# FNet mixing and product-key experts on Trainium2: the terms of token 512 and of column d = 256 as biases, column sums and GpSimd folds

## The chip, the cores and the metric

The kernel runs on one core of one Trainium2 chip. The metric is device time in microseconds (us) of one execution. Five engines work side by side, each in the order of its own instructions: PE (TensorE, the matrix products), ACT (ScalarE), DVE (VectorE), POOL (GpSimd) and SP (SyncE, which here issues most of the transfers). They wait for each other through semaphores.

## The reference

x is [2048 tokens, 512 channels]. Each token is normalised over its channels (xn); the result is the sum of three parts:

```python
a = einsum("bsd,ed->bse", xn, dft_hid_re);  b = einsum("bsd,ed->bse", xn, dft_hid_im)
y = einsum("ts,bse->bte", dft_seq_re, a) - einsum("ts,bse->bte", dft_seq_im, b)   # real part of a 2-D DFT
q = einsum("nd,dhc->nhc", xn, w_q)            # 32 heads, two halves of 128
s1, s2 = q[..., :128] @ k1.T, q[..., 128:] @ k2.T      # 64 scores each; the 2 best of each
# the 2 best of the 4 sums name two rows of u and v; gate by softmax, gelu(xn . u), times v
return x + y + out
```

## The kernel before, in words

**The DFT part** uses the symmetries of the DFT matrices. Tokens are put in an order in which token n, its mirror images and its partners at a distance of 1024 lie in the same lanes, 16 tiles of 128 tokens, four tiles to a group g; the groups are taken in the order G = (1, 0, 2, 3). Sums and differences of partners (`fold`, L356 to L369) leave for each group a quarter of the rows and half of the columns: `Q[0][g]` (even part, 257 columns) and `Q[1][g]` (odd part). `main` (L380 to L391) multiplies them with a quarter of the sequence matrix (`A`), eight fp32 products of 128x512 per call, four PSUM banks `PP[k]`. `evict` copies the banks to SBUF through `turn` (reordering columns), and `hid` (L458 to L474) later multiplies them with the hidden matrix, one tile of 128 output tokens at a time, while the router runs.

**What does not fit the symmetry.** Token 512 is its own mirror image, so it has no place in the 4 x 128 rows: its two partner rows come as `x5` (one partition, two rows of 512). `fold_row` (L371 to L375) folds them on DVE into `s5` (even) and into row 0 of `Q[1][0]` (odd). In `main`, L391 adds token 512's share to the banks of k = 0, h = 0 as two products with one row (a stationary of 1x128 against the one row `c5r` of the sequence matrix). Column d = 256 does not fit the 256 folded columns: `sides` (L400 to L418) sums its products with the matrix on DVE into `a256` (128 x 2 x 512), `sums` (L532 to L545) sums that over the partitions by a product with a column of ones (`one`), two products of 1x512, and turns the result into the row `p256`. In `hid`, L461 adds the column as a product with one row: `pn` (1x128 of p256) against `wrs` (row 256 of the hidden matrix, 1x129). `hid` then copies the bank to SBUF in five ACT pieces (L465 to L469).

**The router** (`scores`, L735 on) multiplies xn, transposed by `xpose` and split into two fp16 parts, with `M[j]` (w_q times the keys, made by `m_mul`, `m_scale` and `m_parts`), 12 fp16 products of 128x512 per tile and head group (L743), 16 tiles times 8 groups j. ACT evicts a bank (L748), DVE finds the best eight per head (L751) and their places (L755). Into this run the nine `hid` calls are placed by hand (`HID`, one per tile from tile 11 of j = 0). **The expert part** (L872 z, L910 g, L955 v) follows. Beside it, `compare`, `compare_w` and `fit` verify that the matrices given have the symmetries used and that the numbers fit in fp16; their flag decides whether a slower general branch, not run here, follows.

**What sets the order.** The code is written for a tile framework whose scheduler orders each engine's instructions by its own estimate of when they become ready; so each engine's order can differ from the text, and once built it is fixed. In the head the layer norm of a group (`ln`) takes four steps on ACT and DVE: means and variances, `Sqrt` on ACT (L315), the reciprocal and its refinement on DVE (L316 to L320), and the normalising of four tiles, mostly on ACT (L332). The groups follow each other closely, so ACT's Sqrt for one group stands between the normalising of the group before and its own. `m_scale` (L196 to L212) needs the largest magnitudes of the four banks `m0` to `m3`, then a reduction over the partitions on GpSimd (L118), before `m_parts` (L219, L220) can write the fp16 parts that the first scores need.

Of the kernel before, what the change touches and what calls it, by code (L numbers as in the profile page):

```python
# [8 lines left out]
F32 = mybir.dt.float32  # L9
# [6 lines left out]
AF = mybir.ActivationFunctionType  # L16
# [3 lines left out]
P = 128  # L20
# [15 lines left out]
def tile_fnet_peer(ctx, tc, x, ca, cb, c5, wt, wf, wr, wq, kt, ut, vn, out):  # L36
# [56 lines left out]
    sums_sb = cst.tile([P, 138 + NF + 3], F32, name="sums")  # L93
    chk, asum = sums_sb[:, 0:70], sums_sb[:, 70:138]
# [5 lines left out]
    fits = sums_sb[:, 138:]  # L100
# [155 lines left out]
    s5 = da.tile([1, 257], F32, name="s5")  # L256
    for t in Q[1]:
        nc.gpsimd.memset(t[:, :, 0:1], 0.0)
# [79 lines left out]
    def fold_d(k, t, f, o):  # L338
# [8 lines left out]
        nc.vector.tensor_tensor(halves(f)[..., 1:P], halves(t[:, :, 0:256])[..., 0:P - 1],  # L347
                          halves(t[:, :, 256:512])[..., 1:P], op=op)
        c = 256 - P * k
        nc.vector.tensor_tensor(o[:, :, c:c + 1], t[:, :, 127:128], t[:, :, 384:385], op=op)  # L350
        if k == 0:
            nc.scalar.activation(f[:, :, 0:P + 1:P], t[:, :, 255:257], AF.Copy)
        nc.vector.tensor_tensor(o[:, :, k:P], f[:, :, k:P], f[:, :, P + k:], op=op)
        nc.vector.tensor_tensor(o[:, :, P + k:2 * P], f[:, :, k:P], f[:, :, P + k:], op=po)
# [16 lines left out]
    def fold_row(k):  # L371

        r = da.tile([P, 2, 512], F32, tag="ft", name=f"r5_{k}", bufs=1).rearrange("p a c -> p (a c)")[0:1].unsqueeze(1)
        nc.vector.tensor_tensor(r[:, 0, 0:512], x5[:, 0], x5[:, 1], op=ALU.subtract if k else ALU.add)
        fold_d(k, r[:, :, 0:512], r[:, :, 512:768], Q[1][0][0:1, 0:1] if k else s5.unsqueeze(1))  # L375
# [3 lines left out]
    def main(k, g):  # L379

        first, last = g == G[0], g == G[-1]
        if first:
            PP[k] = [[pa(f"p{k}_{dt}{h}") for h in range(2)] for dt in range(2)]
        for h in range(2):
            r = A[k, g][:, h * 512:(h + 1) * 512]
            l = Q[k][g][:, h ^ k]
            for dt in range(2):
                nc.tensor.matmul(PP[k][dt][h], l[:, dt * P:(dt + 1) * P], r, start=first, stop=last and h + k > 0)  # L388
                if last and h > k:

                    nc.tensor.matmul(PP[0][dt][0], s5[:, dt * P:(dt + 1) * P], c5r, start=False, stop=True)  # L391

    def add(dst, a, v, first=False):

        if first:
            nc.vector.tensor_scalar(dst, v, a, None, op0=ALU.mult)
        else:
            nc.vector.scalar_tensor_tensor(dst, v, a, dst, op0=ALU.mult, op1=ALU.add)

    def sides():  # L400


        f = FF["t"][:, 0, 0:4]
        nc.vector.tensor_copy(f[:, 0:2], Q[0][G[0]][:, :, 256])
        nc.vector.tensor_copy(f[:, 2:4], c5s[:, :, G[0]])
        for n, g in enumerate(G):
            for h in range(2):
                add(a256[:, h], Q[0][g][:, h, 256:257] if n else f[:, h:h + 1],
                    A[0, g][:, h * 512:(h + 1) * 512], n == 0)
# [5 lines left out]
        nc.scalar.activation(r[:, 0], c5r, AF.Copy, scale=s5[:, 256:257])  # L415
        nc.scalar.activation(r[:, 1, 0:257], s5, AF.Copy, scale=c55)
        nc.gpsimd.tensor_tensor(a256[0:1, 0], a256[0:1, 0], r[:, 0], op=ALU.add)
        nc.gpsimd.tensor_tensor(a5[0:1, 0], a5[0:1, 0], r[:, 1, 0:257], op=ALU.add)  # L418

    PT = {}  # L420
    p256 = uf[12][0:1].rearrange("p (h t) -> p h t", h=2)
    p5 = uf[13][:, 257:263]
    a256 = uf[0].rearrange("p (h t) -> p h t", h=2)
    a5 = uf[1][:, 0:514].rearrange("p (k d) -> p k d", k=2)

    def turn(dst, src):

        d = dst.rearrange("p (q k c) -> p k q c", q=2, k=4)
        v = src.rearrange("p (k q c) -> p k q c", q=2, k=4)
        nc.scalar.activation(d, v, AF.Copy)  # L430

    def evict(k):
        PT[k] = [[uf[8 + 2 * k + dt][:, h * 512:(h + 1) * 512] for h in range(2)] for dt in range(2)]
        for dt in range(2):
            for h in range(2):
                turn(PT[k][dt][h], PP[k][dt][h])
# [21 lines left out]
    def hid(t, n, pre, pn, pim, bank):  # L458

        nc.tensor.matmul(bank[:n, 0:129], pre[0], wfs[:, 0:129], start=True, stop=False)  # L460
        nc.tensor.matmul(bank[:n, 0:129], pn, wrs, start=False, stop=True)  # L461
# [3 lines left out]
        nc.scalar.activation(t[:, 2:256:2], bank[:n, 0:127], AF.Copy)  # L465
        nc.scalar.activation(t[:, 1:256:2], bank[:n, 129:257], AF.Copy)
        nc.scalar.activation(t[:, 256:258], bank[:n, 127:129], AF.Copy)
        nc.scalar.activation(t[:, 513:514], bank[:n, 127:128], AF.Copy)
        nc.scalar.activation(t[:, 0:1], bank[:n, 128:129], AF.Copy)  # L469
# [14 lines left out]
    nc.scalar.dma_start(c5s, c5)  # L484
    c5r = da.tile([1, 512], F32, name="c5r")
# [7 lines left out]
    wrs = uf[13][0:1, 0:129]  # L493
    nc.sync.dma_start(wrs, wr)
# [4 lines left out]
    for n, g in enumerate(G):  # L499
# [5 lines left out]
        if n == 3:  # L505
            fold_row(0)
        main(0, g)
# [10 lines left out]
    for n, g in enumerate(G):  # L518
        fold(1, g)
        if g == 0:  # L520
            fold_row(1)
            nc.scalar.activation(xp[1][0:1], x5, AF.Copy)
# [9 lines left out]
    def sums():  # L532
        for h in range(2):
            p = pc(f"p256_{h}")[0:1]
            nc.tensor.matmul(p, one, a256[:, h], start=True, stop=True)
            turn(p256[:, h], p)
        b5 = pc("b5")
        for k in range(2):
            for dt in range(3 - k):
                c = slice(dt * P, min((dt + 1) * P, 257))  # L540
                n = P if dt < 2 else 1
                nc.tensor.matmul(b5[:n, 3 * k + dt:3 * k + dt + 1], a5[:, k, c], one, start=True, stop=True)
        nc.scalar.activation(p5.rearrange("p (k d) -> p k d", k=2)[:, :, 0:2],
                             b5[:, 0:6].rearrange("p (k d) -> p k d", k=2)[:, :, 0:2], AF.Copy)
        nc.scalar.activation(p5[0:1, 2:3], b5[0:1, 2:3], AF.Copy)  # L545

    def y_rows(n):

        if n == 8:
            hid(uf[13][0:1, 264:778], 1, [p5[:, dt:dt + 1] for dt in range(2)], p5[0:1, 2:3],  # L550
# [4 lines left out]
        hid(uf[n][:, 0:514], P, [PT[0][dt][h][:, c] for dt in range(2)], p256[:, h, c],  # L555
# [19 lines left out]
    def part_b(safe, stS, stP, stE, xt, u_sb, cmp_p):  # L575
# [401 lines left out]
        def compare(n):  # L977
# [37 lines left out]
            if g == 0:  # L1015
# [4 lines left out]
                elif odd == ri:  # L1020
                    nc.vector.memset(t[0:1, 2, 0:2], 0.0)
# [7 lines left out]
        def compare_w(n):  # L1029


            ri, half = divmod(n - 64, 2)
            t = bp.tile([P, 4, 256], F32, tag="w", name=f"cx{n}", bufs=WB)
# [51 lines left out]
        def verdict():  # L1085
# [4 lines left out]
            fm = sums_sb[:, 138 + NF:]  # L1090
# [3 lines left out]
            cols = ((slice(0, 64), 50), (slice(64, 70), 47))  # L1094
# [7 lines left out]
            nc.gpsimd.partition_all_reduce(fr[:, 2:], sums_sb[:, 138:], P, bass_isa.ReduceOp.absmax)  # L1102
# [32 lines left out]
        if not safe:  # L1135
            nc.vector.memset(chk[:, 68:70], 0.0)
# [249 lines left out]
```

## Time and profile before

| | |
|---|---|
| median of 3 runs | 1166.12 us (1165.64 to 1166.95) |
| the profiled execution | 1165.58 us, of which the span from its first to its last instruction is 1163.7 us |
| busy, share of the span | PE 98%, DVE 80%, ACT 52%, POOL 20% |
| granted TensorE clock, mean | 0.997 |
| head: first instruction to the first score product (L743) | 64.0 us |
| scores (L743): busy PE | 297.3 us in 1344 products |
| z (L872) and v (L955): busy PE | 343.0 us and 338.6 us |

The chain of work that ended last is by 72% PE, 16% DVE and 5% POOL. In the rows of the timeline, a row gives start, duration, engine, line, operation, output <- input with shapes, how many were merged, and in square brackets how long the engine had been idle and what ended that. An fp32 product is recorded as two passes, so "x8" of L388 is four products of 128x512.

### The profile page before, as it was taken

To read this page: it belongs to the slowest core of one execution; us is meant where nothing else is said; L and a number is where in the kernel's file an instruction comes from. 1 tells how busy PE (TensorE), PEld (TensorE's weight loads), DVE (VectorE), ACT (ScalarE), POOL (GpSimd) and SP (SyncE) were. 2 spreads that over 40 slices of the span, in tenths; PEclk is the share of its full clock that TensorE was granted. 3 is DMA by queue.
4 is the path that set the end of the run, shared out by engine and by line. 5 is a ranking of instruction groups with operands and counts; after the bars stand their busy time and mean duration, and the time that the engine had idled before them with its cause. 6 is when DMAs were issued, how large, how long until landed. Compare 5 with 4: busy or idle time off the path is not lost.

```text
span 1163.7 us, 25367 instructions
## 1 busy us (share of the span) xinstructions
PE 1142.7 (98%) x9940; PEld 726.3 (62%) x9940; DVE 933.3 (80%) x2845; ACT 608.4 (52%) x1047; POOL 232.3 (20%) x214
## 2 busy tenths in 40 slices
PE   6999999999999999999999999999999999999997
PEld 4455555445445449878479569569569559658763
DVE  7987889798998998983995896797886887788670
ACT  5674576777876745354435435535526436334440
POOL 2032454765756420000010010010010000000000
PEclk9999999999999999999999999999999999999999
DMA  9171334243341204260653653644545555452423
GB/s 366 62 284 55 117 128 172 82 146 117 102 146 44 86 25 129 69 221 20 218 177 111 210 170 135 196 158 162 185 158 173 167 172 168 155 163 60 143 74 103
DMA packets 81296, 163.64 MB, mean 141 GB/s; under 512 B 15876, under 2 KB 31115, under 8 KB 81166
## 3 DMA queue, kind: packets, MB, share of 16 engines
q1 hardware_dynamic: 80864, 161.84, 42.0%
q8 instruction: 80, 1.31, 0.5%
q14 instruction: 50, 0.41, 0.1%
q10 hardware_dynamic: 302, 0.08, 0.0%
HBM read 142.68 MB, written 17.63 MB: 138 GB/s over the span
## 4 chain that ended last, share of the span: by engine, by line
PE 72%; DVE 16%; POOL 5%; ACT 3%; issue 2%; DMA 1%; SPq 0%; POOLq 0%; ACTq 0%; DVEq 0%
PE v L955 28%; PE z L872 27%; PE s L743 8%; DVE vals L751 5%; DVE idx L755 4%; PE g L910 4%; POOL wq L165 1%; PE p L388 1%; DVE m L220 1%; DVE z L694 1%; DVE z L693 1%; POOL wq L166 1%; POOL u L634 1%; PE m L144 1%; ACT wh L158 0%
## 5 line engine op out<-in xcount | busy, mean ns | idle before, releaser
L872 PE MATMUL z<-xb,u 128*128 128x256 f16 (+1 forms) x3840 | 343.0, 251 | 1.3 <-ACT act L879 1.2
L955 PE MATMUL v<-v,act 128*128 128x512 f16 x1536 | 338.6, 379 | 0.0
L872 PEld LDWEIGHTS <-u 128*128 128x128 f16 x3840 | 309.8, 98 | 28.0 <-issue 1.7
L743 PE MATMUL s<-m,xq 128*128 128x512 f16 x1344 | 297.3, 379 | 0.0
L955 PEld LDWEIGHTS <-act 128*128 128x128 f16 x1536 | 147.3, 98 | 171.0
L743 PEld LDWEIGHTS <-xq 128*128 128x128 f16 x1344 | 129.6, 98 | 150.4 <-issue 0.2
L900 DVE TENSOR_TENSOR L<-io_lam,cmp 128x2048 f16<-128x2048 f16 x128 | 155.7, 1217 | 61.8 <-PE g L910 61.8
L879 ACT ACTIVATE act<-z,scl 128x256 f32<-128x256 f32 (+1 forms) x224 | 100.8, 498 | 172.3 <-PE z L872 172.2
L751 DVE MAX8 vals<-ss 128x8 f32<-128x64 f32 x1024 | 152.7, 216 | 20.1 <-ACT ss L748 19.9
L968 POOL TENSOR_TENSOR y<-y,xr 128x512 f32<-128x512 f32 x15 | 27.5, 1836 | 610.9 <-DMA y<-y_d 459.3
L925 ACT ACTIVATE act<-w 128x1024 f16<-128x1024 f32 x52 | 69.6, 1354 | 93.0 <-DVE w L918 92.4
L755 DVE FIND_INDEX8 idx<-vals,ss 128x8 uint16<-128x256 f32 x256 | 107.2, 419 | 0.0
L918 DVE SCALAR_TENSOR_TENSOR w<-act,scl,g 128x1024 f32<-128x1024 f32 x64 | 81.0, 1274 | 29.7 <-ACT act L879 29.7
L748 ACT ACTIVATE ss<-s,wsc 128x512 f32<-128x512 f32 x112 | 74.5, 679 | 49.1 <-PE s L743 39.7
L1027 ACT ACTIVATE cx<-cx 128x896 f32<-128x896 f32 x64 | 60.5, 946 | 74.0 <-DVE cx L1011 54.0
L926 DVE TENSOR_TENSOR act<-w,act 128x1024 f16<-128x1024 f32 x64 | 86.0, 1346 | 4.1 <-ACT act L925 4.1
L1005 DVE TENSOR_TENSOR cx<-cx 128x512 f32<-128x512 f32 (+2 forms) x84 | 48.4, 610 | 24.0 <-DMA cx<-in_cb_dram 23.1
L910 PEld LDWEIGHTS <-L 128*128 128x128 f16 x2048 | 60.6, 96 | 11.2 <-DVE R L908 1.3
L910 PE MATMUL g<-R,L 128*128 128x32 f16 x2048 | 61.7, 176 | 0.3 <-DVE R L908 0.2
L908 DVE TENSOR_TENSOR R<-R,cmp 128x512 f16<-128x512 f16 x128 | 59.6, 465 | 1.5
L166 POOL TENSOR_TENSOR wq<-wq,wh 128x1024 f16<-128x1024 f32 x26 | 55.4, 2132 | 11.1 <-DVE xq L456 7.2
L905 DVE TENSOR_TENSOR R<-io_c,cmp 128x512 f16<-128x512 f16 x128 | 53.3, 416 | 0.0
(285 smaller groups left out, 1081.4 us busy)
## 6 DMA issues: line engine op xcount, KB each, us to landing
v<-v_d SPq DMA_DIRECT2D x67, 512.0 KB, 4.1
cx<-in_cb_dram SPq DMA_DIRECT2D x64, 448.0 KB, 4.5
wq<-in_wq_dram SPq DMA_DIRECT2D x32, 512.0 KB, 5.4
fit<-in_wq_dram SPq DMA_DIRECT2D x28, 512.0 KB, 5.1
uv<-in_vn_dram SPq DMA_DIRECT2D x16, 512.0 KB, 3.8
uv<-in_ut_dram SPq DMA_DIRECT2D x16, 512.0 KB, 5.8
c<-in_ca_dram SPq DMA_DIRECT2D x8, 512.0 KB, 11.2
y<-y_d SPq DMA_DIRECT2D x16, 256.0 KB, 2.6
```

Source lines behind the costliest of these rows:

```text
L743: nc.tensor.matmul(ps, xt[i][:, l, kd, :], m[:, r, kd, :], start=(n == 0), stop=(n == 3 * KD - 1))
L748: nc.scalar.activation(s.rearrange("p g e -> p (g e)"), ps, AF.Copy, scale=inv)
L751: nc.vector.max(vals[:, i, w, :, h], s[:, g, :])
L755: nc.vector.max_index(idx[:, i, w].rearrange("p k h -> p (k h)"), vals[:, i, w, 0:2].rearrange("p k h -> p (k h)"), s[:, w * HC:g + 1, :]. ...
L872: nc.tensor.matmul(ps if n == 1 else ps.rearrange("p (b n) -> p b n", b=2), ug[:, l, c % 2, kd, :], xb2[:, k0, r, kd, :] if n == 1 else xb ...
L879: nc.scalar.activation(ACT[bb][:, cg * m:cg * m + m, :], pv[:, i], AF.Gelu_apprx_tanh, scale=zsc)
L900: nc.vector.tensor_tensor(L.rearrange("p t (l two) -> p t l two", two=2), io_lam.rearrange("p (l two) -> p l two", two=2).unsqueeze(1).to_ ...
L910: nc.tensor.matmul(p[:, hf, t * NC:(t + 1) * NC], L[:, t, :], R[:, t, :], start=True, stop=True)
L918: nc.vector.scalar_tensor_tensor(w, act[:, :, ts], fw, p.rearrange("p h (n c) -> p c (h n)", c=NC), op0=ALU.mult, op1=ALU.mult)
L925: nc.scalar.activation(w16[..., 0], w, AF.Copy)
L926: nc.vector.tensor_tensor(w16[..., 1], w, w16[..., 0], op=ALU.subtract)
L955: nc.tensor.matmul(pv, w16[:, c, :, l], v_sb[g][:, r, cc, :], start=(n + cc == 0 and k == 0), stop=(n == 15 and cc == 1 and k == 2))
```

## The change

1. **Token 512 in the evictions.** L391 is gone. The two values of its matrix row that occur (`c52`, a copy of the first two of `c5r`) are multiplied with `s5` on ACT (`spread`, two products of 1x256), written to DRAM (`s5_d`) and read back as columns (`s5c`, 128 x 2 x 2), both by GpSimd's queue. `turn` gets a bias: for the banks of k = 0, h = 0 it runs twice on every other column, as Identity with the bias `s5c`.
2. **Column 256.** `sides` writes the last group's step in the turned order (four steps of 128x256 for two of 128x512) into another tile. `sums` takes eight products with `a256`'s columns as stationary and two columns `w2` (the two values of row 256 of the hidden matrix, loaded to all partitions) as moving operand, into one bank, and evicts it once: `p256` is now a column pair per tile. `hid` loses L461 and adds the pair as bias: six ACT pieces for five, five of them Identity with a bias.
3. **Row folds on GpSimd.** `fold_row` runs on GpSimd, in tiles of its own, for k = 0 and k = 1 one after the other in the text where only k = 0 stood; row 0 of `Q[1][0]` is then copied by DVE from `s5i`.
4. **The verification** covers what is now assumed (that these rows hold two values in turn): four memsets become small additions, and one 1x129 row is loaded and compared, by two DVE steps and one ACT step. One ACT copy (`c52`) now stands first on ACT, with a table load of its own ahead of the one for Sqrt.

```diff
     def fold_row(k):
-        r = da.tile([P, 2, 512], F32, tag="ft", name=f"r5_{k}", bufs=1).rearrange("p a c -> p (a c)")[0:1].unsqueeze(1)
-        nc.vector.tensor_tensor(r[:, 0, 0:512], x5[:, 0], x5[:, 1], op=ALU.subtract if k else ALU.add)
-        fold_d(k, r[:, :, 0:512], r[:, :, 512:768], Q[1][0][0:1, 0:1] if k else s5.unsqueeze(1))
+        r = da.tile([1, 1, 768], F32, tag="r5", name=f"r5_{k}", bufs=1)
+        nc.gpsimd.tensor_tensor(r[:, 0, 0:512], x5[:, 0], x5[:, 1], op=ALU.subtract if k else ALU.add)
+        fold_d(k, r[:, :, 0:512], r[:, :, 512:768], (s5i if k else s5).unsqueeze(1), nc.gpsimd)
+    def spread():
+        for a in range(2):
+            nc.scalar.activation(s5p[:, a].rearrange("o t p -> o (t p)"), s5[:, 0:256], AF.Copy, scale=c52[:, a:a + 1])
+        nc.gpsimd.dma_start(s5_d.rearrange("n p -> (n p)").unsqueeze(0), s5p.rearrange("o a t p -> o (a t p)"))
+        nc.gpsimd.dma_start(s5c.rearrange("p a t -> p (a t)"), s5_d.rearrange("n p -> p n"), allow_slow_non_contiguous=True)
...
-                nc.tensor.matmul(PP[k][dt][h], l[:, dt * P:(dt + 1) * P], r, start=first, stop=last and h + k > 0)
-                if last and h > k:
-                    nc.tensor.matmul(PP[0][dt][0], s5[:, dt * P:(dt + 1) * P], c5r, start=False, stop=True)
+                nc.tensor.matmul(PP[k][dt][h], l[:, dt * P:(dt + 1) * P], r, start=first, stop=last)
...
+        for a in range(2):
+            nc.scalar.activation(d[..., a::2], v[..., a::2], AF.Identity, bias=b[:, a:a + 1])
...
-        nc.tensor.matmul(bank[:n, 0:129], pre[0], wfs[:, 0:129], start=True, stop=False)
-        nc.tensor.matmul(bank[:n, 0:129], pn, wrs, start=False, stop=True)
+        nc.tensor.matmul(bank[:n, 0:129], pre[0], wfs[:, 0:129], start=True, stop=True)
...
-        nc.scalar.activation(t[:, 2:256:2], bank[:n, 0:127], AF.Copy)
+        for d, v, a in ((t[:, 2:256:4], bank[:n, 0:127:2], 0), (t[:, 4:256:4], bank[:n, 1:127:2], 1),
+                        (t[:, 256:258], bank[:n, 127:129], 1), (t[:, 513:514], bank[:n, 127:128], 1),
+                        (t[:, 0:1], bank[:n, 128:129], 1)):
+            nc.scalar.activation(d, v, AF.Identity, bias=pn[:, a:a + 1])
...
+    nc.scalar.activation(c52, c5r[:, 0:2], AF.Copy)
...
-        for h in range(2):
-            p = pc(f"p256_{h}")[0:1]
-            nc.tensor.matmul(p, one, a256[:, h], start=True, stop=True)
-            turn(p256[:, h], p)
+        b8 = pc("b8")
+        for n in range(8):
+            g, q = divmod(n, 2)
+            c = q * 256 + g % 2 * P
+            nc.tensor.matmul(b8[:, 2 * n:2 * n + 2], a256[:, g // 2, c:c + P], w2, start=True, stop=True)
+        nc.scalar.activation(p256, b8[:, 0:16].rearrange("p (n a) -> p n a", n=8), AF.Copy)
```

The scheduler places the new steps as follows. **ACT in the head.** `xb` and `xq_113` are the tiles of group 0 that are being normalised, `ff_0` takes group 2's Sqrt, `nm` a zero for the statistics of group 3. Before:

```order
L332 ACTIVATE xb_109<-xb_109,negm,rstd 128x512
L332 ACTIVATE xq_113<-xq_113,nm_163 128x512
L295 ACTIVATE nm_163<-xq_113 128x1
L315 ACTIVATE ff_0_309<-mvs,eps 128x4
L352 ACTIVATE ff_0_309<-ft_0_328 128x4
L332 ACTIVATE xq_116<-xq_116,negm,rstd 128x512
```

With the change (its own line numbers; L316 is its Sqrt, L385 the two products of `spread`, `r_0` the row fold's tile):

```order
L333 ACTIVATE xb_109<-xb_109,negm,rstd 128x512
L333 ACTIVATE xq_113<-xq_113,nm_164 128x512
L353 ACTIVATE r_0_395<-r_0_395 1x2
L435 ACTIVATE r_628<-c5r,s_156 1x4x2x64
L296 ACTIVATE nm_164<-xq_113 128x1
L385 ACTIVATE s5p<-s_156,c_197 1x256
L385 ACTIVATE s5p<-s_156,c_197 1x256
L436 ACTIVATE r_628<-s_156,c_199 1x257
L316 ACTIVATE ff_0_316<-mvs,eps 128x4
L353 ACTIVATE ff_0_316<-ft_0_335 128x4
L333 ACTIVATE xq_116<-xq_116,negm,rstd 128x512
```

Five ACT steps that read what GpSimd's row fold writes (`r_0`, and `s` for s5) moved ahead of group 2's Sqrt; before, their like stood behind group 3's normalising. **GpSimd** with the change, from the normalising of x5 (before, the reduction of L118 followed it directly):

```order
L336 TENSOR_SCALAR x_162<-x_162,mvs,rstd 1x512
L375 TENSOR_TENSOR r_0_395<-x_162 1x512
L348 TENSOR_TENSOR r_0_395<-r_0_395 1x2x127
L351 TENSOR_TENSOR s_156<-r_0_395 1x1
L354 TENSOR_TENSOR s_156<-r_0_395 1x128
L355 TENSOR_TENSOR s_156<-r_0_395 1x128
L375 TENSOR_TENSOR r_1_406<-x_162 1x512
L355 TENSOR_TENSOR s5i<-r_1_406 1x127
L386 DMA s_d<-s5p 16x1x32
L387 DMA s5c<-s_d 128x4x1
L118 ISA pw_432<-mx_423 128x3
```

(Three rows of the second fold, like those of the first, are left out ahead of its last.) Both folds now stand ahead of the two transfers of s5c. **DVE around group 3's last fold step**, which makes `q_3`, the operand of the last products of k = 0; `ft_1` is the first fold step of k = 1. Before, then with the change:

```order
L354 TENSOR_TENSOR fo_3_379<-ff_3_378 128x2x128
L374 TENSOR_TENSOR r_0_388<-x_161 1x512
L368 TENSOR_TENSOR q_3_151<-fo_3_379 128x257
L369 TENSOR_TENSOR q_3_151<-fo_3_379 128x257
L347 TENSOR_TENSOR r_0_388<-r_0_388 1x2x127
```

```order
L355 TENSOR_TENSOR fo_3_386<-ff_3_385 128x2x128
L366 TENSOR_TENSOR ft_1_454<-xq_114,xq_115 128x1024
L369 TENSOR_TENSOR q_3_151<-fo_3_386 128x257
L370 TENSOR_TENSOR q_3_151<-fo_3_386 128x257
L348 TENSOR_TENSOR ff_1_455<-ft_1_454 128x4x127
```

The step of 128x1024 took the place of the row step of 1x512 ahead of q_3.

More of the change, by code (lines that the diff above doesn't have):

```diff
@@ L92, in tile_fnet_peer @@
     NF = NW + 32 + NCH - 1
-    sums_sb = cst.tile([P, 138 + NF + 3], F32, name="sums")
-    chk, asum = sums_sb[:, 0:70], sums_sb[:, 70:138]
+    sums_sb = cst.tile([P, 139 + NF + 3], F32, name="sums")
+    chk, asum = sums_sb[:, 0:71], sums_sb[:, 71:139]
     wsc = cst.tile([P, 5], F32, name="wsc")
@@ L256, in tile_fnet_peer @@
     s5 = da.tile([1, 257], F32, name="s5")
+    s5i = da.tile([1, 257], F32, name="s5i")
     for t in Q[1]:
@@ L506, in tile_fnet_peer @@
             fold_row(0)
+            spread()
+            fold_row(1)
         main(0, g)
@@ L554, in y_rows @@
         h, c = g // 2, slice(q * 256 + g % 2 * P, q * 256 + g % 2 * P + P)
-        hid(uf[n][:, 0:514], P, [PT[0][dt][h][:, c] for dt in range(2)], p256[:, h, c],
+        hid(uf[n][:, 0:514], P, [PT[0][dt][h][:, c] for dt in range(2)], p256[:, n],
             [PT[1][dt][h][:, c] for dt in range(2)], (pb if q else pc)(f"hy{q}_{g}"))
@@ L1135, in part_b @@
         if not safe:
-            nc.vector.memset(chk[:, 68:70], 0.0)
+            nc.vector.memset(chk[:, 68:71], 0.0)
         for g in range(3):
```

83 lines of the change are left out of this document (55 added, 28 removed).

## The prediction

> **What bounds the kernel now.** I read the page's head first, then the waits, then the head of the program in order of time.
>
> ```profile
> span 1163.7 us, 25367 instructions
> PE 1142.7 (98%) x9940; PEld 726.3 (62%) x9940; DVE 933.3 (80%) x2845; ACT 608.4 (52%) x1047; POOL 232.3 (20%) x214
> PE m L148 <- DMA wq<-in_wq_dram: 8.8, 1, 8.8
> PE p L388 <- DVE q L368: 3.9, 2, 3.3
> DVE vals L751 <- ACT ss L748: 19.9, 20, 3.3
> ```
>
> PE is idle for only 21 us of the span: 8.8 at the start, 3.9 for the folds of the head; most of the rest is the tail after its last product. From the first score at 64 us on it waits for almost nothing. So a PE slot taken out behind 64 us is time won, if DVE follows; DVE waited 19.9 us for the scores' evictions, spread over 20 places, so it has the slack to follow a few us. In the head it is otherwise: PE waits for DVE, and DVE for ACT. So the change has two halves, a gain behind 100 us on PE, and a head whose chain it lengthens.
>
> **The head.** This is the timeline before, rows of POOL, ACT, DVE and PE:
>
> ```profile
> 17.21 4.21 POOL L335 TENSOR_SCALAR x<-x,mvs,rstd 1x512 f32<-1x512 f32 x2 [3.21 <-DVE rstd L319]
> 20.41 0.30 ACT L315 ACTIVATE ff<-mvs,eps 128x4 f32<-128x4 f32 x1
> 21.45 0.17 DVE L316 RECIPROCAL ff<-ff 128x4 f32<-128x4 f32 x1
> 24.39 3.70 PE L388 MATMUL p<-c,q 128*128 128x512 f32 x8 [0.53 <-DVE q L368]
> 31.41 7.91 PE L388 MATMUL p<-c,q 128*128 128x512 f32 x14 [3.32 <-DVE q L368]
> 35.23 0.67 DVE L374 TENSOR_TENSOR r<-x 1x512 f32<-1x512 f32 x1
> 35.83 0.41 DVE L368 TENSOR_TENSOR q<-fo 128x257 f32<-128x257 f32 x1
> 36.29 0.48 PEld L388 LDWEIGHTS p<-c,q 128*128 128x128 f32 x2 [0.38 <-DVE q L368]
> 42.45 7.10 PE L388 MATMUL p<-c,q 128*128 128x512 f32 x16
> 64.03 1.24 PE L743 MATMUL s<-m,xb 128*128 128x512 f16 x5
> ```
>
> GpSimd has x5 normalised at 21.42. ACT takes group 2's Sqrt at 20.41, DVE its reciprocal at 21.45; the products of groups 2 and 3 wait for what follows from it (3.32 and 0.38 us idle). With the change ACT's queue holds five steps ahead of this Sqrt, the last three of which need s5 complete. So the Sqrt cannot come before GpSimd has folded the row. What that takes, by size:
>
> ```profile
> L681 POOL TENSOR_TENSOR c<-vals 128x64 f32<-128x64 f32 x7 | 2.2, 319 | 10.4 <-DVE vals L751 10.4
> L706 POOL TENSOR_TENSOR di<-if 128x128 f32<-128x128 f32 x7 | 3.2, 458 | 0.0
> L418 POOL TENSOR_TENSOR u<-u,r 1x257 f32<-1x257 f32 x1 | 0.7, 718 | 0.0
> L166 POOL TENSOR_TENSOR wq<-wq,wh 128x1024 f16<-128x1024 f32 x26 | 55.4, 2132 | 11.1 <-DVE xq L456 7.2
> L416 ACT ACTIVATE r<-s,c 1x257 f32<-1x257 f32 x1 | 0.5, 493 | 0.0
> ```
>
> From 64 to 128 columns 139 ns are added, 2.2 ns a column, and 128 to 257 agree; so 512, 254, 1, 128 and 128 columns take 1.28, 0.71, 0.18, 0.46 and 0.46 us, 3.1 in all: s5 at 24.5. Then ACT's two products of 1x256 and the one of 1x257 at some 0.4 each from start to start (L416's 0.49 less the overlap of neighbours): Sqrt at 25.8, reciprocal at 26.15, **4.7 us later** than now. Bounds: at L166's 2.1 ns a column without a fixed part the fold takes 2.1 (delay 3.7); at L335's 2.1 us per 512 it takes 4.2 and more (delay 6.2). I take 4.7, the four rows with two operands being nearest. Nothing hides it: DVE's queue stands at this reciprocal, and the normalising of group 2, q_0, q_2 and q_3 are behind.
>
> Group 3's q_3 is another 0.55 later: DVE has the fold of 128x1024 (1.23 a step, some 1.15 from start to start) ahead of it where the row step took 0.60 (35.23 to 35.83). So the last group's products begin at 36.29 + 4.7 + 0.55 = 41.55. From there PE is the bound again, with less to do:
>
> ```profile
> 39.32 1.05 PE p L391 x2
> 40.37 1.06 PE p L388 x2
> 41.43 1.06 PE p L391 x2
> 57.99 0.23 PE xp L452
> 63.31 0.87 PE xp L447 x8
> ```
>
> The chain of waits shows the one-row products at 1.05 and 1.06, both gone. What is left from the last group's first product to the first score: 8 + 32 passes at 0.434 (16 in 6.95, 42.45 to 49.40), 17.4; ten transposed tiles at 0.44 (two of four steps each in the last row's 0.87), 4.4; eight L452 at 0.23, 1.8: 23.6 us. Now it takes 27.74 (36.29 to 64.03) with the 2.1 of L391, so 2.0 are stalls, of which 0.5 lie beside L391. Stepping the new order through ACT and DVE by these rows I find 0.4; between 0.4 and 1.5 I take 1.0. First score at 41.55 + 23.6 + 1.0 = 66.15: **the head loses 2.1 us**; 0.6 less or 0.5 more by the stalls, 1.0 less or 1.5 more by the fold. DVE's own row steps (0.60 for the first of five) are inside this: from 41.55 on PE is the bound, so taking them off DVE wins nothing by itself.
>
> Three new things lie beside it. ACT's first step waits for c5r, then loads a second table; a load is 1.28 us, and the first Sqrt now begins at 7.78:
>
> ```profile
> 7.78 0.30 ACT L315 ACTIVATE sm<-mvs,eps 128x4 f32<-128x4 f32 x1 [2.57 <-DVE mvs L311]
> L315 ACT ACT_TABLE_LOAD x1 | 1.3, 1283 | 3.9 <-issue 3.9
> k_sb<-in_kt_dram ACTq DMA_DIRECT2D x1, 64.0 KB, 2.4
> wq<-in_wq_dram SPq DMA_DIRECT2D x32, 512.0 KB, 5.4
> c<-in_ca_dram SPq DMA_DIRECT2D x8, 512.0 KB, 11.2
> 2.79 0.61 ACTq L266 DMA_DIRECT2D c5r<-in_cb_dram  x1
> ```
>
> If c5r lands as k_sb on the same queue, 2.4 us after issue, the copy is done at 5.4 and the table at 6.7: hidden. At the wq loads' 5.4 Sqrt is 1.9 late. I take 0. The transfers of s5c: GpSimd does the second fold first (24.5 + 3.1 = 27.6), then issues two in a row; ACT needs the columns when the first bank is complete, at 41.55 + 0.87 = 42.4. At k_sb's 2.4 each they land at 32.4, hidden by ten us; the 11.2 of the large loads is the other end, a rival below. Splitting four evictions costs ACT 0.1 a piece, inside the stalls.
>
> **Behind 64 us.** The chain of waits, `hid` for one tile and `sums`:
>
> ```profile
> 98.50 1.81 PE p L535 x4
> 100.31 1.19 PE b L542 x10
> 104.42 0.31 PE hy L461 x2
> 108.17 0.22 PE hy L460 x2
> 108.39 0.41 PE hy L461 x2
> 108.80 0.42 PE hy L462 x2
> 109.22 0.22 PE hy L463 x2
> 109.44 0.22 PE hy L464 x2
> ```
>
> L461 holds the chain for 0.41, and the product behind it for 0.42, though it is of the same size as L464 at 0.22: its weight load comes only when L461 has run. Without L461 I expect L462 at 0.22, so 0.61 a tile, eight tiles, 4.9, and 0.4 for the ninth (0.31 and some 0.1): **5.3 won**. The least is L461's own slots, 8 x 0.41 + 0.31 = 3.6. [...] ACT's sixth piece and the biases cost at most 0.8 a tile on an engine that is idle half of the time there. DVE's four steps per tile stay.
>
> `sums`: 1.81 go; 16 passes come, each like one of L542's ten in 1.19, so 1.9: **0.1 lost**, or up to 1.2 if each pass takes the 0.19 of its weight load.
>
> The verification beside the expert part (one small load on SP, two DVE steps and one ACT step) I cost at nothing: PE's products hide it, and if DVE stood for the load's landing, some 3 us, PE's z products would cover that too.
>
> **The sum.** 2.1 + 0 - 5.3 + 0.1 = -3.1. The profiled execution took 1165.58, of which 1163.7 is span, 0.54 under the median of 1166.12; 1165.58 - 3.1 = 1162.5, and on the scale of the median **1163.0**, 0.27% less. 0.2%, 2.3 us, is about what a measurement of this kernel can tell from no change.
>
> **Rivals.** *Only L461's own slots go* (the change takes out less PE time than it seems: L462 keeps its 0.42): 2.1 - 3.6 + 0.1 = -1.4, 1164.7. For it: the trace has no `hid` without L461. Against: L463 and L464 at 0.22.
>
> *The head costs more.* The fold at L335's rate, a late table, or the TensorE clock. The clock shows here:
>
> ```profile
> 30.00:40.00 10.00, 8.59 (x16) 3.51 (x16) 8.99 (x23) 5.87 (x14) 0.00 (x0) 0.83 0.13 49
> ```
>
> After 3.32 us of idling it is 0.83 in this window, 1.7 us lost. The new idle times are 23.86 to 29.1 (slow products of group 0 follow, which the next wait of 1.9 hides) and twice some 2 us ahead of groups 2 and 3. If one of these slowed group 3's products, 1.7 are added. [...] Any of the three adds 1.5 to 1.9, 1164.5 to 1164.9; two of them 1166.4.
>
> *The other side: s5c comes late.* If each transfer takes the 11.2 us of the large loads, they land at 27.6 + 22.4 = 50.0, ACT stands 7.6 us at the first eviction, with the four maxima of `m_scale` behind it, and PE's products of k = 1 wait for the banks: 1163.0 + 7.6 = 1170.6. It decides from a landing at 42.4 + 3.1 + 2.4 = 47.9 on. Against it: between 30 and 40 us the transfers move 49 GB/s, so the queues are nearly empty.
>
> *The head loses less*: if fold and stalls come out at their lower ends, the head loses 0.5, 1161.4.
>
> **How the numbers follow.** Forecast 50%, its own range 1161.8 to 1164.3; only the own slots 16%; head dearer 17% (1164 to 1167); late s5c 8%; head cheaper 9%. Leaving out the late half of s5c and the outermost ends, the range is 1160.2 to 1168.0. Faster by over 0.2% (up to 1163.8): most of the forecast, the cheap head and a little of the next two, 0.56; within 0.2%, 0.33; slower (from 1168.4), s5c and two dear heads together, 0.11.
>
> **What would show it.** Right: L316's reciprocal for group 2 near 26, with ACT's wait for POOL ahead of it; the first score near 66; in `hid` four products at 0.22 each and no 0.42; PE without waits behind. Wrong: the reciprocal at 21 to 22 (no stall), or ACT idle at the first eviction until a DMA; DVE waiting no more for scores, so that PE's gain stops there.

## The result, and the profile after

| | before | with the change |
|---|---|---|
| median (12 runs each, taken together) | 1166.14 us (1165.05 to 1167.72) | 1166.03 us (1163.65 to 1169.27) |
| ratio | | 0.9997, 95% interval 0.9987 to 1.0006 |
| profiled execution, its span | 1165.58, 1163.7 us | 1163.72, 1161.9 us |
| first score product | 64.03 us | 69.10 us |
| first z product | 434.66 us | 434.25 us |

No difference that can be measured, where 3 us less were forecast. The profiled execution with the change is among the fastest of its twelve, so I compare the two traces by stages and not by their ends. These are the heads of its page and of its waits (engine, line, releaser: us in all, times, longest):

```profile
span 1161.9 us, 25370 instructions
PE 1135.6 (98%) x9930; PEld 724.4 (62%) x9930; DVE 933.6 (80%) x2840; ACT 614.6 (53%) x1063; POOL 238.2 (21%) x226
```

```profile
PE p L400 <- DVE q L369: 9.7, 3, 6.8
PE m L148 <- DMA wq<-in_wq_dram: 9.6, 1, 9.6
DVE vals L784 <- ACT ss L781: 12.3, 15, 3.0
```

PE has 7.1 us less to do (1142.7 to 1135.6), and it waits 5.8 us longer for the folds of the head (3.9 to 9.7, the longest 6.8 where it was 3.3). Those two rows are most of the result; the rest is where the wait comes from. The timeline of the head, rows of ACT, POOL, DVE and PE (start, duration, engine, line, what, count, and in brackets the idle time ahead and what ended it):

```profile
2.80 0.61 ACTq L267 DMA_DIRECT2D c5r<-in_cb_dram  x1
...
3.92 1.28 ACT L514 ACT_TABLE_LOAD   x1 [3.92 <-issue]
8.65 0.20 ACT L514 ACTIVATE c<-c5r 1x2 f32<-1x2 f32 x1 [3.44 <-DMA c5r<-in_cb_dram]
8.87 1.28 ACT L316 ACT_TABLE_LOAD   x1
10.16 0.30 ACT L316 ACTIVATE sm<-mvs,eps 128x4 f32<-128x4 f32 x1
...
23.79 1.26 POOL L375 TENSOR_TENSOR r<-x 1x512 f32<-1x512 f32 x1
25.93 0.72 ACT L435 ACTIVATE r<-c5r,s 1x512 f32<-1x512 f32 x1 [0.65 <-POOL s L351]
27.97 0.28 ACT L316 ACTIVATE ff<-mvs,eps 128x4 f32<-128x4 f32 x1
28.29 0.18 DVE L317 RECIPROCAL ff<-ff 128x4 f32<-128x4 f32 x1 [3.22 <-ACT ff L316]
29.38 0.38 DVE L321 SCALAR_TENSOR_TENSOR negm<-mvs,rstd 128x4 f32<-128x4 f32 x1
...
31.74 5.86 PE L400 MATMUL p<-c,q 128*128 128x512 f32 x8 [6.79 <-DVE q L369]
44.19 12.87 PE L400 MATMUL p<-c,q 128*128 128x512 f32 x28 [1.72 <-DVE q L369]
69.10 1.24 PE L776 MATMUL s<-m,xb 128*128 128x512 f16 x5
```

Two delays follow each other. First, ACT stands at the copy of `c52` until c5r has landed, 5.85 us after its issue began, and then loads the second table: the first Sqrt comes at 10.16 where it came at 7.78, **2.4 us late**, and everything behind it with it. Second, ACT's steps that read the row fold stand ahead of group 2's Sqrt, as forecast. (The DVE step at 29.38, 0.38 us for 0.16 before, belongs to a third, small one; e5_both and e7_nofold explain it.) In `hid` the chain shows four products at 0.22 and no 0.41 or 0.42; the first row is the eight two-column products of `sums`:

```profile
103.58 1.68 PE b L565 x16
...
112.64 0.22 PE hy L485 x2
112.86 0.22 PE hy L486 x2
113.08 0.22 PE hy L487 x2
113.30 0.22 PE hy L488 x2
```

For comparison with the kernel before, this is the row there in which the expert part begins:

```profile
434.66 5.52 PE L872 MATMUL z<-xb,u 128*128 128x128 f16 x96
```

From the first score to the first z it took 434.66 - 64.03 = 370.63 us, now 434.25 - 69.10 = 365.15: **5.5 us won** behind the head, **5.1 lost** in it. What is left of the 1.9 us between the two profiled executions lies behind the first z; there the traces of this study scatter by 2.8 us (721.1 to 723.9 from the last score to the last product) in no order that follows the kernels.

### The profile page after: what moved, and what is told of

Its sections match the earlier page's. It is cut to its first block, busy times and chain, and to the rows that moved or that the text cites. A ratio compares the mean times of both kernels' runs of the same rounds, so it can differ in the third digit from the quotient of the medians.

```text
span 1161.9 us, 25370 instructions
## 1 busy us (share of the span) xinstructions
PE 1135.6 (98%) x9930; PEld 724.4 (62%) x9930; DVE 933.6 (80%) x2840; ACT 614.6 (53%) x1063; POOL 238.2 (21%) x226
## 4 chain that ended last, share of the span: by engine, by line
PE 94%; DVE 2%; ACT 1%; POOL 1%; DMA 1%; issue 0%; ACTq 0%
PE z L905 29%; PE s L776 29%; PE v L988 28%; PE g L943 4%; PE m L144 2%; PE p L400 2%; ACT xq L333 1%; DMA c5r<-in_cb_dram 1%; PE xp L472 0%; DVE L L933 0%; DVE ft L366 0%; POOL x L336 0%; DVE act L959 0%; DVE w L951 0%; PE hy L485 0%
```

## The experiments

The theory after this result: *part 2 wins 5.5 us in `hid`; parts 1 and 3 lose 5.1 in the head, of which 2.4 are the copy of `c52`, the rest ACT's wait for the row fold.* The main rival: the profiled execution misleads, and what was won in `hid` is lost again behind it. All runs in one table; the ratio is to runs of the kernel before on the same chip, with its 95% interval, the two middle columns are from the profile:

| run | first score | first z less first score | ratio | median us |
|---|---|---|---|---|
| before | 64.03 | 370.63 | | 1166.14 |
| the change | 69.10 | 365.15 | 0.9997 (0.9987 to 1.0006) | 1166.03 |
| e1_hid: part 2 alone | 64.02 | 364.99 | 0.9942 (0.9928 to 0.9955) | 1159.67 |
| e2_head: parts 1 and 3 alone | 68.85 | 370.64 | 1.0030 (1.0018 to 1.0041) | 1169.69 |
| e3_c52 | 66.64 | 366.78 | 0.9984 (0.9975 to 0.9993) | 1164.43 |
| e5_both | 64.92 | 365.15 | 0.9961 (0.9947 to 0.9975) | 1161.70 |
| e6_full | 64.15 | 367.37 | 0.9976 (0.9967 to 0.9986) | 1162.72 |
| e7_nofold | 62.33 | 366.81 | 0.9951 (0.9934 to 0.9969) | 1160.26 |
| e8_split | 64.03 | 365.00 | 0.9952 (0.9939 to 0.9966) | 1159.40 |
| e9_triple | 65.55 | 371.77 | 1.0021 (1.0012 to 1.0031) | 1167.92 |
| e10_late | 63.76 | 365.24 | 0.9945 (0.9930 to 0.9960) | 1159.00 |

### Each half by itself

**Part 2 alone** (e1_hid): the kernel before with the new `hid`, `sums`, `sides`, `w2` and its verification.

```diff
-        nc.tensor.matmul(bank[:n, 0:129], pre[0], wfs[:, 0:129], start=True, stop=False)
-        nc.tensor.matmul(bank[:n, 0:129], pn, wrs, start=False, stop=True)
+        nc.tensor.matmul(bank[:n, 0:129], pre[0], wfs[:, 0:129], start=True, stop=True)
...
+            nc.scalar.activation(d, v, AF.Identity, bias=pn[:, a:a + 1])
```

> Part 2 of the change alone (column 256 by two-column sums and as a bias in hid, with its verification); token 512 and the row folds stay as before. Theory 1 (hid wins what was forecast, and the head of the changed kernel eats it): first score at 64.0 as before, four hid products of 0.22 each, 5.3 us less than before, a ratio near 0.9955. Theory 2 (the slots that PE wins in the scores are given back where the expert part begins, since DVE or ACT end last there): the same 0.22 in hid, but 0 to 2 us less, a ratio of 0.998 to 1.0, and idle time of PE between 435 and 450 us.

The timeline has the first score where it was and the z products 5.6 us earlier:

```profile
64.02 1.46 PE L759 MATMUL s<-m,xb 128*128 128x512 f16 x6
429.01 11.16 PE L888 MATMUL z<-xb,u 128*128 128x128 f16 x197
```

The ratio of 0.9942 is 6.8 us, its interval 5.2 to 8.4: nothing that `hid` wins is given back. Theory 2 falls.

**Parts 1 and 3 alone** (e2_head): the changed kernel with the `hid`, `sums` and `sides` of before.

```diff
+        nc.tensor.matmul(bank[:n, 0:129], pn, wrs, start=False, stop=True)
...
-        for n in range(8):
-            nc.tensor.matmul(b8[:, 2 * n:2 * n + 2], a256[:, g // 2, c:c + P], w2, start=True, stop=True)
+        for h in range(2):
+            nc.tensor.matmul(p, one, a256[:, h], start=True, stop=True)
```

> Parts 1 and 3 alone (token 512 as a bias in the evictions, row folds on GpSimd, the copy c52 first on ACT); hid and the sums of column 256 as before. Theory 1: first score at 69.1 as in the changed kernel, nothing won behind it, 5.1 us more than before, a ratio near 1.0044. Theory 2 (the head's delay is swallowed later and what the changed kernel lacks is lost elsewhere): first score at 69.1, but 0 to 2 us more than before, a ratio of 1.0 to 1.0017.

The first score is at 68.85, and from there to z it takes 370.64 us, as before. The trace so says 4.8 us lost, the times 3.5 (2.1 to 4.8). Theory 1 holds in its mechanism; the size by the times is a little under it. The two halves add to -0.8 us by the traces and to some -3 by the medians, against -0.1 for the whole; the medians' own intervals cover some 2 us of that difference, and the last us has no explanation here.

### Where the head's 5 us come from

**The copy of c52 away from ACT** (e3_c52):

```diff
-    nc.scalar.activation(c52, c5r[:, 0:2], AF.Copy)
+    nc.gpsimd.tensor_copy(c52, c5r[:, 0:2])
```

> The changed kernel, with the copy c52 on GpSimd, so that ACT begins with the Sqrt as before. Theory 1 (of the head's 5.1 us, 2.4 are ACT's wait for c5r and the second table load, the rest is ACT's wait for the row fold): first Sqrt back at 7.8, group 2's Sqrt near 24.7, first score between 66 and 67, 2.4 to 3 us less than the changed kernel, a ratio to before near 0.9977. Rival (the row fold's wait alone decides, the early delay is hidden under it): first Sqrt at 7.8, first score still at 68.5 to 69, ratio near 1.0. If the wait for c5r is also what makes the changed kernel's times spread over 5.6 us, the spread here is near the 2.7 us of the kernel before.

From its timeline:

```profile
7.95 0.30 ACT L316 ACTIVATE sm<-mvs,eps 128x4 f32<-128x4 f32 x1 [2.71 <-DVE mvs L312]
23.84 0.72 ACT L435 ACTIVATE r<-c5r,s 1x512 f32<-1x512 f32 x1 [0.65 <-POOL s L351]
24.46 0.28 ACT L316 ACTIVATE ff<-mvs,eps 128x4 f32<-128x4 f32 x1
66.64 1.24 PE L776 MATMUL s<-m,xb 128*128 128x512 f16 x5
```

The first score comes 2.46 us earlier than with the change. That this equals the 2.4 of the early wait is partly luck, since the scheduler changed the order too: only two of the five steps now stand ahead of group 2's Sqrt. The row fold of s5 ends 2.1 us earlier (24.64 against 26.73), which is what the early wait is worth up to there; the Sqrt then comes 3.5 us earlier, since three steps moved behind it; and of that 1.0 is lost again on DVE. From its reciprocal at 24.78 to the end of `negm` (the shift of the normalising, L317 to L321) DVE takes 2.49 us here, 1.47 with the change and 0.95 before; GpSimd's second fold runs beside it in both (24.72 to 28.17 here). What that does to DVE is the subject of the next two runs. So the 2.6 us of loss that are left are ACT's wait for GpSimd and DVE's slow steps together, and not the wait alone, as theory 1 had it. The times are 1.9 us under before (0.8 to 2.9), where the head's 2.6 and the 5.5 won behind it would give 2.9. The profiled execution took 366.78 us from the first score to the first z, 1.6 more than the change. The windows of one us there (busy time of PE, PEld, DVE, ACT, POOL, then the granted clock):

```profile
104.00:105.00 1.00, 1.00 (x6) 0.46 (x5) 0.24 (x1) 0.14 (x2) 0.00 (x0) 1.00 0.09 16
105.00:106.00 1.00, 1.00 (x4) 0.40 (x3) 0.00 (x0) 0.00 (x0) 0.00 (x0) 0.52 0.00 0
106.00:107.00 1.00, 1.00 (x4) 0.34 (x3) 0.00 (x0) 0.00 (x0) 0.00 (x0) 0.50 0.00 0
107.00:108.00 1.00, 1.00 (x4) 0.18 (x3) 0.00 (x0) 0.16 (x1) 0.00 (x0) 0.50 0.00 0
108.00:109.00 1.00, 1.00 (x8) 0.54 (x6) 0.44 (x4) 0.92 (x3) 0.00 (x0) 0.77 0.00 0
```

PE is busy throughout, and yet the clock is at half for 3.4 us. I come back to that below. My guess that the wait for c5r makes the times spread was wrong: they spread over 4.1 us here too, and those of the kernel before, taken beside them, over 4.2.

**No ACT step waits for GpSimd** (e5_both): e3_c52, and the fold's copy, the spread and the two rows of `sides` on GpSimd.

```diff
-            nc.scalar.activation(f[:, :, 0:P + 1:P], t[:, :, 255:257], AF.Copy)
+            e.tensor_copy(f[:, :, 0:P + 1:P], t[:, :, 255:257])
...
-            nc.scalar.activation(s5p[:, a].rearrange("o t p -> o (t p)"), s5[:, 0:256], AF.Copy, scale=c52[:, a:a + 1])
+            nc.gpsimd.tensor_scalar(s5p[:, a].rearrange("o t p -> o (t p)"), s5[:, 0:256], c52[:, a:a + 1], None, op0=ALU.mult)
...
-        nc.scalar.activation(turned(r[:, 0]), halved(c5r), AF.Copy, scale=s5[:, 256:257])
+        nc.gpsimd.tensor_scalar(turned(r[:, 0]), halved(c5r), s5[:, 256:257], None, op0=ALU.mult)
```

> The changed kernel, with the copy c52 on GpSimd and with every ACT step that reads the row fold on GpSimd too (the fold's copy of two values, the two products for the spread, the two rows for sides), so that nothing on ACT waits for GpSimd. Theory 1: group 2's Sqrt at 20.4 and its reciprocal at 21.5 as before, first score at 62 (before's 64.0 less the 2.1 of the one-row products), 7 us less than before, 1159, a ratio near 0.994. Rival (with the one-row products gone PE waits in their place for the last group's folds and for s5c): first score at 64, ratio near 0.9955. If s5c is late now that GpSimd has more to do ahead of its transfers, ACT stands at the first eviction and the ratio is 0.997 or above.

The first score is at 64.92, not 62: theory 1 has its sign right and misses 2.9 us (0.9961 is 4.5 us under before, as the 0.9 lost in the head and the 5.5 won behind it give). The reciprocal is at 21.3, as it should be. What comes behind it is not; DVE and GpSimd in the timeline:

```profile
21.35 1.26 POOL L378 TENSOR_TENSOR r<-x 1x512 f32<-1x512 f32 x1
21.40 1.23 DVE L351 TENSOR_TENSOR fo<-ft 128x2 f32<-128x2 f32 x1
22.69 0.62 POOL L348 TENSOR_TENSOR r<-r 1x254 f32<-1x254 f32 x1
22.74 0.60 DVE L319 SCALAR_TENSOR_TENSOR ff<-ff 128x4 f32<-128x4 f32 x1
...
34.82 15.88 PE L403 MATMUL p<-c,q 128*128 128x512 f32 x32 [3.65 <-DVE q L372]
```

A DVE step of two columns takes 1.23 us, and it ends with GpSimd's fold step beside it (22.63 and 22.61); the next takes 0.60 and ends with GpSimd's next (23.34 and 23.31). In the kernel before the same two (L350 and L318 there) take 0.16. DVE's reciprocal, which has one operand, kept its 0.18 beside such a step with the change (28.29, in GpSimd's 28.14 to 28.76). Nor did GpSimd's normalising of x5, with one tensor operand, hold DVE up: it runs until 21.27 in e5_both, and DVE's step of 128x1024 with two inputs beside it runs from 20.14 in its usual 1.23. So the fold costs twice: ACT's wait for it, and DVE's longer steps beside it.

**The fold left out** (e7_nofold): e5_both without both row folds and the spread, zeros in their place.

```diff
+    nc.gpsimd.memset(s5, 0.0)
...
-            fold_row(0)
-            spread()
-            fold_row(1)
```

> The kernel of e5_both with both row folds and the spread left out (their results are zeros, so token 512's share is left out of y): GpSimd has nothing to do between the normalising of x5 and the reduction over the partitions; ACT, PE and DVE keep their instructions. Theory 1 (in e5_both the head lost because GpSimd's steps and DVE's steps of two operands exclude each other: the DVE step of 128x2 took 1.23 us beside GpSimd's first fold step where it took 0.17 before): DVE's steps keep their times of before, group 3's first product 3 us earlier than in e5_both, first score at 62, a ratio near 0.9937. Rival (the head is bound by PE's own work or by ACT once the one-row products are gone): first score at 64 to 65 as in e5_both, ratio 0.996.

```profile
22.06 0.16 DVE L353 TENSOR_TENSOR fo<-ft 128x2 f32<-128x2 f32 x1
31.92 3.70 PE L406 MATMUL p<-c,q 128*128 128x512 f32 x8 [2.68 <-DVE q L374]
37.34 12.94 PE L406 MATMUL p<-c,q 128*128 128x512 f32 x28 [1.72 <-DVE q L374]
62.33 1.24 PE L778 MATMUL s<-m,xb 128*128 128x512 f16 x5
```

DVE's step is back at 0.16, group 2's products begin 2.9 us earlier than in e5_both (31.92 against 34.82), and the first score is at 62.33 as theory 1 expected. In these two executions GpSimd's fold beside DVE so costs 2.9 us at group 2 and 2.6 at the first score, though no ACT step waits for its result. The half clock that followed e5_both's longer wait (0.59 between 36 and 40 us; 32 passes in 15.88 us, where at 0.434 they take 13.9) is no part of it: from group 2's first product to the first score e5_both takes 30.1 us, and e7_nofold, at full clock but with a wait of 1.72 for group 3, 30.4. The times do not tell the two kernels apart (0.9951, 0.9934 to 0.9969, against 0.9961, 0.9947 to 0.9975). (This profile too has the half clock behind `sums`, for 3.4 us from 99.2 on: 366.81 from first score to first z, 1.8 more than e1_hid.)

### Why hid wins more than its products

**A product of full height for the one-row product** (e6_full): before, with one line of `hid` changed.

```diff
-        nc.tensor.matmul(bank[:n, 0:129], pn, wrs, start=False, stop=True)
+        nc.tensor.matmul(bank[:n, 0:129], pre[0], wfs[:, 0:129], start=False, stop=True)
```

> The kernel before, with the one-row product of column 256 in hid (stationary 1x128, moving 1x129) replaced by a second product of the full size (stationary 128x128, moving 128x129, the same operands as the product ahead of it); column 256 is so left out of y. As many products as before. Theory 1 (the loss is the change of the tile's height: the product behind a one-row stationary waits until that has run): five products of 0.22 each, so 8 x (0.41 + 0.42 - 0.44) = 3.1 us less than before, a ratio near 0.9973. Rival (the loss is the second write into the same bank, or simply the product): 0.41 and 0.42 stay, ratio 1.0.

The chain of one tile:

```profile
108.12 0.22 PE hy L460 x2
108.34 0.22 PE hy L461 x2
108.57 0.22 PE hy L462 x2
108.79 0.22 PE hy L463 x2
109.01 0.23 PE hy L464 x2
```

With the same number of products and the same second write into the bank, both the 0.41 and the 0.42 are gone: 367.37 from first score to first z, 3.3 less than before, and 2.8 (1.6 to 3.8) by the times. So 3.3 us of L461's cost were the change of height, not the product: some 0.2 us at each change (0.41 and 0.42 for 0.22). Taking it out altogether (e1_hid) gives the other 2.4, of which nine products at 0.22 are 2.0.

### The half clock behind sums

`sums` in the new form is 2.8 us of products with one or two columns. Two kernels on e1_hid: its two halves, now `sums5` and `sums8`, **in two places** (e8_split), and the eight products **three times over** (e9_triple).

```diff
-                if j == 0 and i == 10 and not safe:
-                    sums()
+                if j == 0 and i in (10, 11) and not safe:
+                    (sums5, sums8)[i - 10]()
```

> The kernel of e1_hid with the small products of sums in two places, the five for a5 behind tile 10 and the eight two-column ones behind tile 11, where all stood behind tile 10. Theory 1 (3 us of products with one or two columns in one stretch count as little work, so that the clock falls to half for some 3.4 us in some runs, as in the profile of e3_c52 behind them): no such fall, mean clocks of 0.998 to 1.0 as before where e1_hid's were 0.996 to 0.999, 0.5 to 1.7 us less than e1_hid, a ratio near 0.9935. Rival (the fall has nothing to do with them): clocks and times as in e1_hid, ratio 0.9942.

```diff
-        for n in range(8):
+        for n in 3 * list(range(8)):
```

> The kernel of e1_hid with the eight two-column products of sums issued three times over, so that 6.7 us in one stretch hold nothing but products of one or two columns. Theory 1 (little work lowers the clock): 3.7 us of slots more than e1_hid, and in every run the clock falls to 0.5 for one or two windows of 3.4 us in or behind the stretch, some 1.7 to 3.4 us more; 5.4 to 7 us more than e1_hid in all, a ratio near 0.999 to 1.0. Rival (PE's being busy is what counts, whatever the size): 3.7 us more and the clock at 1.0 there, a ratio near 0.9973.

The windows of e9_triple, two us each, through the stretch (99.9 to 107.9) and behind it, show the fall that theory 1 expected:

```profile
102.00:104.00 2.00, 2.00 (x20) 2.00 (x20) 0.94 (x6) 0.00 (x0) 0.00 (x0) 1.00 0.03 8
104.00:106.00 2.00, 2.00 (x12) 2.00 (x12) 0.00 (x0) 0.00 (x0) 0.00 (x0) 0.52 0.00 0
106.00:108.00 2.00, 2.00 (x11) 1.81 (x12) 0.00 (x0) 0.26 (x3) 0.00 (x0) 0.50 0.00 0
108.00:110.00 2.00, 2.00 (x6) 0.76 (x5) 0.00 (x0) 0.14 (x2) 0.00 (x0) 0.50 0.00 0
110.00:112.00 2.00, 2.00 (x9) 0.63 (x7) 0.00 (x0) 0.00 (x0) 0.00 (x0) 0.77 0.00 0
```

Half clock from 104 to 110.9 with PE busy all along, and 371.77 from first score to first z, 6.8 more than e1_hid: 3.4 of slots (the eight products take 1.68, and there are two more sets of them) and 3.4 of clock (half of the 6.8 us). By the times it is 8.2 us over e1_hid, more than the 5.4 to 7 expected. Another 1.5 is in this execution's head (65.55), which had a lower clock too (0.57 between 32 and 36 us); whether that is the rest in the other runs, the record does not say. The mean clocks of all ten runs, 0.992 to 0.997 against 0.996 to 0.999 of e1_hid, go the same way. So here small products, some 8 us of them back to back, brought the clock to half although PE was busy throughout. The head of the change fits that: its clock falls at 25.9 us (0.94 between 25 and 26, then 0.50), 0.9 us after PE's last products of 64 columns (L148, back to back from 21.27 to 24.95). Behind the 2.8 us of `sums` in one stretch the profiles of e3_c52 and e7_nofold have the fall, 3.4 us at half clock each, and those of the change, e1_hid and e5_both have none (1.00 throughout); what decides between them, no run here shows.

Whether splitting helps is not shown: e8_split's mean clocks were 0.995 to 1.000 in five runs against 0.996 to 0.999, its profile has no fall, its median is 0.3 us under e1_hid's and its ratio 0.0010 above, all within what the runs scatter. e1_hid's own profile had no fall either.

### A version that takes token 512 out of the head

e10_late is e8_split without L391, both row folds on DVE, the one for s5 behind `sides`, and the columns added to the evicted blocks beside tiles 9 and 10:

```diff
-        if n == 3:
-            fold_row(0)
...
+    fold_row(0)
+    spread()
     sides()
...
+            nc.scalar.activation(v[:, a::2], v[:, a::2], AF.Identity, bias=at[:, a:a + 1])
```

> The kernel of e8_split with token 512 taken out of the head: no one-row products, both row folds on DVE, the first of them (s5) behind the sums of sides, the spread behind it, and its columns added to the two evicted blocks by four ACT steps beside tiles 9 and 10 of the scores, well ahead of hid; nothing of it on GpSimd but the two transfers and the copy c52. Theory 1 (the head's cost in the changed kernel is where the fold stands and on what engine, not that it is done): first score at 62 to 62.5 as in e7_nofold, nothing lost behind it, 1.5 to 2 us less than e8_split, a ratio near 0.9935. Rival (DVE and ACT are so full between 60 and 100 us that the steps come out of the scores' evictions and PE waits): first score at 62, but 0 to 2 us more than e8_split and idle time of PE between 62 and 115 us, ratio 0.995 to 0.997.

Neither: the first score is at 63.76, and nothing is lost behind it (365.24). A window (clock in the third column from the end) and the timeline show a wait and a half clock:

```profile
32.00:36.00 4.00, 4.00 (x6) 1.72 (x7) 3.13 (x7) 1.15 (x3) 0.00 (x0) 0.58 0.03 6
```

```profile
31.89 16.27 PE L406 MATMUL p<-c,q 128*128 128x512 f32 x32 [3.32 <-DVE q L368]
49.92 1.31 PE L474 MATMUL xp<-ident,xq 128*128 128x128 f32 x8 [1.76 <-DVE m L220]
63.76 1.46 PE L777 MATMUL s<-m,xb 128*128 128x512 f16 x6
```

PE now waits 1.76 us for `m_parts` ahead of its transposes, nearly as long as the 2.1 us that L391 took before; from that step to the first score it takes 13.8 us, as in e1_hid (50.26 to 64.02). `m_parts` ends a chain through ACT's evictions and maxima, GpSimd and DVE that is here longer than PE's own. So of the 2.1 us of one-row products taken out, 1.76 came back as this wait. The order of PE's products has a part in it. In e7_nofold the DVE step of `m_parts` is no earlier (49.3 against 49.1 for its first), and yet PE does not wait there: from group 2's first product on it has 36 passes of `main` ahead of the transposes (8 and 28 above), here 32, and four passes at 0.434 are 1.7 us. With that order e10_late might come near e7_nofold's 62.33; it was not run. The half clock at 32 to 36 us, behind a wait of 3.3, can delay the evictions and so the chain too; how much, one profile does not say. e1_hid, e8_split and e10_late are the fastest kernels of this study, 1159.0 to 1159.7 us, and cannot be told apart.

## Why the prediction was right in the main, and where it was wrong

It forecast 1163.0 us; the time was 1166.03, within the range given but not faster. One term of its sum was put at nothing and measured 2.4 us, one mechanism in the head, worth 0.5 us, was not seen, and the others were right. Point by point:

- **The second table and c5r.** The step "Sqrt is 1.9 late. I take 0" failed. Of the two landings that it weighed, 2.4 us as for k_sb on the same queue and 5.4 as for the wq loads, the second came about: 5.85. With the table load behind it that is 2.4 us on the first Sqrt, and 2.1 to 2.3 of it are still there where GpSimd normalises x5 and folds the row (19.48 for 17.21; 26.73 for e3_c52's 24.64). The range had a late table as a rival (1164.5 to 1164.9). k_sb was a poor neighbour: it is issued first, while c5r comes fourth on its queue, with the large loads already on their way (with the change the share of the DMA engines is 0.34 up to 3 us and 1.01 from 3 to 6); which of the two makes it land late, no run shows.
- **The row fold and the reciprocal.** Forecast 26.15; measured 28.29, less the 2.4 above 25.9. The fold took 2.94 us (23.79 to 26.73), forecast 3.1. Right. What was not seen is that the DVE steps behind the reciprocal run beside GpSimd's second fold: up to the end of `negm` they take 1.47 us, where it was 0.95.
- **The last group's products.** Forecast 41.55; 44.19 less 2.4 is 41.8. Right in size, with some luck: from the reciprocal on it took 15.9 us for the 15.4 forecast, which are DVE's 0.5, and the reciprocal less the 2.4 was 0.3 early.
- **From there to the first score.** Forecast 24.6, measured 24.9. Right: PE waits for nothing there. e10_late shows a limit of it: with an undelayed head and another order of its products PE waited for `m_parts`, and most of L391's 2.1 us came out as that wait.
- **s5c.** Hidden, as forecast: ACT read it at 45.35 without waiting. The landing, forecast at 32.4, was at some 36.3: GpSimd waited 3.16 us for the first transfer before it issued the second (at 33.67, 2.6 to landing).
- **hid and sums.** Forecast -5.3 and +0.1, measured together -5.5 (`sums` 2.79 us for 3.00, so -0.2); e6_full shows that 3.3 of it are the change of height. The rival that only L461's own slots go is out.
- **The verification.** Nothing of it is seen in any wait of PE. Right.
- **The clock in the head.** The forecast was that group 0's slow products (5.86 where 3.70 are usual) are hidden by the next wait; they are (1.17 us of idling follow). That waits of some 2 us cost no clock, as the sum without such a term has it, no run had shown; the two ahead of groups 2 and 3, 1.17 and 1.72 us with the change, left the clock at 1.00. The fall itself did not need the idle time that the prediction reckoned with: it came 0.9 us into the wait. That the clock could fall behind `sums` was not thought of; the change's own profile does not have it (1.00 from 98 to 112 us).

With 2.4 in place of 0 the sum is -0.7 us, 1165.4, and the trace's own balance is -0.4. DVE's longer steps beside GpSimd's folds cost no more than 0.5 us in this kernel, because during the first fold DVE waits for ACT anyway; it is what stands in the way as soon as that wait is taken out (e5_both).

## What to carry to other kernels

A small step that is first in an engine's queue holds back everything behind it until its operand lands: here the copy of `c52` waited for c5r until 5.85 us after that transfer's issue began, and the first Sqrt came 2.4 us late. The 2.4 us of k_sb on the same queue was no measure of that landing; and if the step's function needs a table load of its own, that counts too (1.28 us here). Work that moves to an idle engine can cost by the queues that wait for it and by what runs beside it; here it did both, with 2.53 and 0.65 us of ACT idle ahead of the first two steps that read the fold, and with a DVE step of 0.16 us that took 1.23 (e5_both). And before a PE product in a head is counted as a gain, follow the other chain that ends in the same place: if it is as long, the product's slot becomes a wait (1.76 of 2.1 us in e10_late), unless the order puts other products there.

## What the runs showed of the hardware

- A stationary of 1x128 between ones of 128x128 cost some 0.2 us at each change: five products took 0.22 each once all had full height, where two of them had taken 0.41 and 0.42.
- GpSimd steps with two operands, of one row only, and DVE steps with two operands took longer beside each other: DVE steps of 0.16 us took 1.23 and 0.60 and ended within 0.03 us of GpSimd's (e5_both), and GpSimd steps of 1x128, 0.44 and 0.45 while DVE was idle (the change), took 0.53 and 0.63 there. A DVE reciprocal, with one operand, kept its 0.18 beside a GpSimd step of 0.62 (the change), and DVE's step of 128x1024 its 1.23 beside GpSimd's normalising, with one tensor operand (e5_both).
- Some 8 us of products of one or two columns, back to back, brought the granted clock to 0.5 for 6.8 us while PE was busy (e9_triple); 2.8 us of them were followed by 0.5 for 3.4 us in two of the five profiles that have them in one stretch (e3_c52, e7_nofold). In the head of the change 3.7 us of products of 64 columns and 0.9 us of idling were followed by 0.50.
